# Neighbour rows of a speech codec kernel: 29 transposing loads from HBM replaced by transfers inside SBUF, and new instruction queues

## The chip, the cores and the metric

The kernel runs on one core of one Trainium2 chip. The metric is the device time of one execution in microseconds (us). The engines have these names in the text and in the profile: PE is TensorE (matrix products), DVE is VectorE, ACT is ScalarE, POOL is GpSimd, and SP is SyncE, which here does nothing but issue transfers. HBM is the chip's large memory, SBUF the core's working memory of 128 partitions, PSUM the eight banks that PE writes.

## The reference

A speech codec's core: a three-tap convolution along time for each of 512 channels, SiLU, four rounds of residual vector quantization with eight entries each, and a second three-tap convolution over the sum of the picked entries. `x` is 2 x 16000 x 512 in bf16.

```python
xp = jnp.pad(x, ((0,0),(pad,pad),(0,0)))
z = jnp.zeros_like(x)
for i in range(K):                                   # K = 3
    z = z + xp[:, i:i+T, :] * dw_enc[i][None, None, :]
z = _silu(z)
res = z
q = jnp.zeros_like(z)
for s in range(Nq):                                  # Nq = 4, codebooks of C = 8 rows
    cb = codebooks[s]
    d2 = jnp.einsum("btd,btd->bt", res, res)[..., None] - 2.0 * jnp.einsum("btd,cd->btc", res, cb) + jnp.einsum("cd,cd->c", cb, cb)[None, None, :]
    idx = d2.argmin(-1)
    sel = cb[idx]
    q = q + sel
    res = res - sel
qp = jnp.pad(q, ((0,0),(pad,pad),(0,0)))
y = jnp.zeros_like(x)
for i in range(K):
    y = y + qp[:, i:i+T, :] * dw_dec[i][None, None, :]
return y
```

## The kernel before

**Tiles.** Each of the two sequences is cut into nine tiles (18 in all, numbered 0 to 17). A tile has G groups of 128 rows: G is 6 and 8 for the two tiles at the outer ends and 16 for the rest. Neighbouring tiles overlap by two rows. Partition p of a tile holds the G consecutive rows p*G to p*G+G-1, so that "group g" is the set of rows p*G+g for all p.

**The transposed input and its halo.** The first convolution wants channels on the partitions. So the tile lies transposed in a buffer `XT` of 128 channels x 4 blocks of channels x 18 slots x 128 columns. Slot g+1 holds group g, and column p of a slot is row p*G+g. The tap before group 0 needs the row in front of each p*G, and the tap behind group G-1 the row behind each p*G+G-1. Slot 0 (the halo before) and slot G+1 (the halo behind) hold them. The row in front of p*G is row (p-1)*G+G-1, which is column p-1 of slot G: slot 0 is slot G shifted by one column, and slot G+1 is slot 1 shifted by one column the other way. Only one column of each cannot be had in this way: column 0 of slot 0 and column 127 of slot G+1 are rows outside the tile, which feed only rows that the overlap lets the neighbour tile compute.

**Loading.** Tiles 0 and 1 come by two plain transfers (L569), are turned by PE and copied into `XT1` (L580, L590). Every later tile is loaded by `load`: G transposing transfers from HBM (L599), one for each group, and two for the halo, each a further transposing transfer of the same size from HBM, whose rows start one row earlier (L607, 15 of them) or one row later (L613, 14 of them). Where a tile touches the start or the end of a sequence, POOL makes the halo instead: a fill with zeros (L609, L615) and a copy of the shifted slot (L610, L616). All these transfers are issued by SP. There are two buffers `XT0` and `XT1`, used in turn, so the loads of tile n can start only when the last tap of tile n-2 has read the buffer.

**What follows for a tile.** Each tile is worked in two halves of two channel blocks.
- `front`: the three taps, one multiplication with `WENC` each, on ACT (L640) or DVE (L641) into `TA` and `TB`; two sums on DVE (all DVE operations on two tensors are recorded at L393); exponential on ACT (L646); plus one on ACT (L647) or DVE (L648).
- `front2`: reciprocal on ACT (L658) and the gate product on DVE (L393), which gives `ZB`.
- `select`: PE multiplies `ZB` with the codebooks and itself (L677, 8064 small products); small DVE steps decide the first three entries of every row.
- `resid`: PE subtracts the picked entries from `ZB` in PSUM (L835, L840); copies on ACT (L862) or DVE (L863) bring the result back; scores for the fourth entry and its decision.
- `back`: the second convolution as PE products of one-hot rows with weighted codebooks (L912, L914, L916), copies from PSUM into one of four output buffers `YB` (L921 on ACT, L922 on DVE), and the store (L949), issued by SP.
PE also runs products that nobody reads while it would be idle (L969, "fillers").

**What sets the order.** The program does not issue its steps as the loops go. Each step is given to a class `Plan` with its engine (or a choice of ACT and DVE), an assumed duration ("cost"), the tokens that it reads and writes, and for a transfer a "tail", the assumed time until it has landed. The order on each of the five queues is baked into the string `RANK`, two digits for each step, and the choice between ACT and DVE into the string `WHERE`. `Plan.order` replays the five queues with the assumed costs only to merge them into one sequence and to place the fillers. In that replay a step waits for an earlier one in this way:

```python
end = t + c + s["tail"]
...
at[u] = max(at[u], t + c + self.AGAIN[e] if ue == e else end + self.LATENCY[e])
```

For a step on another engine the tail counts; for a step on the same engine it does not, and `AGAIN["SP"]` is 0. In the built program each queue keeps its order, and every dependence between two engines, or on a transfer, is a semaphore wait of the dependent instruction.

Of the kernel before, what the change touches and what calls it, by code (L numbers as in the profile page):

```python
# [185 lines left out]
def kernel(  # L186
# [33 lines left out]
    RANK = ("00010300000501090M0f0a0N080K0e010b030f0X0l0e0i0b0U0h0q0s000o000q0A0b0d0n0E040s0708020f0a0e060g0109040607090d0f0i0j02080a"  # L220
            "0c0e0g0h0m05050d070709020406040a0c0608010b0i0r03020A0H0K0v050c0T0V0Y1115191b0q0E0F0c0G0r0j0m0o1e1m1p1d1o1u0h0o0t1j1w1y0p"
            "0d0k0m030i0t0z0F0H0J0L0P0S0g0j0l0p0k0v0D0y0I0B0O0x0l130u0m0u0G0w0C0j1i0p1r0n1l0k1g0Q0h0g0R0W100Z120n1f171614181a1h1c1k0w"
            "0z0y1A0B1E0r0s1M1O1N1P1Q1R1S0k0t0L0u1T1V1X1Z1W1Y202122230l0v250w242628292a2b2c2d0n0x0P0y0z2i2j0A0B0T0R0C0D2n2m0E0F0U0V0G"
            "0H2t2A2D2H2J0K120N170P191m0M141t1s1n1q0x1t1x1v1z0D271B1C1D0C1F1G1H1I0J0O0h050b0708030i0g0a0604090c0f020j0l0d1L0I1J1K1U0M"
            "0N2e0Q2l0S2w0W2v0X2x0I0J2z2B2C2E2G2I2K0o0L130O2M2N2O2R2T2W2X2Y2Z300p0Q330R31343637383a3b3c0q0S3e0T0U3i3j0V0W3l1b0X0Y1d3n"
            "0Z101e3o11123t3w3x3z3B151l1c1t1f1u1p191n1a1o1f2h2k2f2g2o2p2q2r102L0t0o0B0u0k0m0e0q0A0n0z0r0p0v0x0s0y0w0Z2s0Y2u2y2F112P16"
            "182U152V2S3239353d1a3p1c3r1g3F1i3E13143D16173I3L3K3N3P3Q3S0r1d1p1g3U3W3Y403V3Z414243440s1i471j464a4c4b4d4e4f4g0u1k1v1l1m"
            "1x1y1n1o1z1A1p1q1D4u1r1s1C4x1v1w4H1x1z4Q4V4X4Z531L1P1S1Y2024211R1X1W221Y1Q1W1Y201Z1P1V1V2627181b3R1e1h3X48454k4l4p4s0t1t"
            "4z1u4v4w4y4A4C4D4E4F4G4I0v1y4L1A4J4K4M4P4R4S4U4W0w1D1J1F1G541M1I1J1O1N1K1M1S1R1N1O1U1T1T1Z5C21225F5H5J5L5O265W29282b2a2f"
            "2a292e2b2u2q2l2A2r2t2r2n2x2q2p0G0O0Q0E0D0T0M0I0N0C0R0F0K0J0P0H0S0L3k3g3h3f3m1f3q3s1k491h3v3u3y3A1j3C3H1q4m15110Y1a0Z0W17"  # L230
            "100V161912181c14130X0U3M3J3O1m3T1r1s4h1w4o1B4B1E4N1G4Y1B1C511E1H565a585c5e5h2Q5j0y1U5s1X5l5n5p5r5w5y5A5E5G5I0z235M245K5N"
            "5R5Q5T5Y60630C2d652f2g2e2d2h2i6e2f2l2m2i2h2n2o2j2k2t2v6C2u2z6L6N6P6T702I732S2G327D2K2L2C2M2E2C2N2D2R2F2F2U2H312O2N4n4i4q"
            "4j4r1F4t4O1K571h1i1b1v1u1s1g1d1r1x1w1o1n1l1e1q1k1j504T1I1H521L55591Q5o5d5f5g5b5i5m5k5q1Z5B215P255Z276425275V282c676b6a6d"
            "6f6h3G6j0D2p6r2s6m6o6q6s6u6v6w6x6y6z0E2w2o2y6A6D6F6E6G6H6I6J0F2B2s2D2F2w2x2G2H2z2v2J2K2A2B2V2Y2K7v33357J38397Q7S7W7Y813g"
            "2W3k303m312W3j2Z3w373b3n323l353d3o8j3q38342j2k6k2C2E6S6W6V7274767a0H2Q7f2T7c7e7g7i7j7k7m7o7q7s0I2Z2J307t7u7y7x7z7A7B7C0J"
            "347F36372P2Q3b3c2U2T3e3f2V2X3h3i2Y893p3r8h3t3v8n8p8r8t8A3G8I413u423w3z3N3l3U3o3r403t3P3v3v3O3m3Q3p3E1C1F1I1E1P1G1A1z1y1O"
            "1M1B1H1N1D1L1K1J5u5v5x5t5z235D5S2c6B625X615U6669686c2g6t1U1X251V1T1R292a1S26222820231Q241W0x0A6l6g6n6i6p2p2m6K2t6X2u752y"
            "772I7H2O2P7d2W2X7n7r7p7w7E7G7I0K3a2R3d7K7M7N7O7V7X7Z8486880L3s343u8b8f8i8l8o8q8s8u0M3x8x3y3z3a3c3C3D3h3d3E3H3i3f3J3K3j3k"
            "3T3V983W3Y9e9j9l9n9q453y4l3L4g3N3M4h3J4p3M3L4d3E4q3Q3Q4s3P4t3S3S6Q6O6M6R6U6Y6Z712M7L2n2d2c2i2e2j2k2l2h2w2m2g2b2q2o2r0B0G"
            "2s787b797h7l2L2N7P2S837R7T807U8285878a338w368y398G3b8H3A3B8F3F3I8K8O8N8Q8S8U8V0N3R8X3S8Y909295919497999a9b0O3X3r3Z9d9f9h"  # L240
            "9g9i9k9m9o0P439r46473z3A484a3C3F4b4c9F3D4e4f3G3H4i4j9R4m4na4a7a9abad4xak4B3U4C3V494A3T4F3X3Y4E3W4Gaz414W484R4c4g3L3M8R44"
            "499y9C9A9E9J9M9O0Q4k9U4o9Q9T9W9Z9Ya3a6aaacae0R4wag4zahajamanaparasau0U4Daw4H4I3Z404J4K41424L4M43464O4PaQ454S4Tb14X4Ybabd"
            "bgbjbn594h5c4k5f4n4E5e4p5n4u4z5g4o5r4A4H5k4r5o4t4B2L2A2I2G2J2E2z2M2y2x2v2D2R2B2Q2P2O2H8d8e8g8c8k8v8m8z3e8M8E8B8C8D8J3g8L"
            "8P3n9c30352Y36372U3a38323c33392S2V312Z2X2T938Z8W8T963s3q9p3x9x3B9H3I9V3Ka14r4uaf4v4yalaqaoataxaBaD0S4NaM4QaGaIaKaNaRaTaU"
            "aVaWaX0T4UaZ4VaYb0b2b3b4b5b6b70W4Z4a5152bi4d55564g4f585a4j4i5b5d4m4l5h5lbK5i5pbNbQbTbVbY5F4G5J4N5P4P4I5I4L5X4U4Q5O4O5S4R"
            "4N5Q4Q5T4T4R9u9s9t9v9w9B9z9D3Oai3l3s3f3h3t3i3g3w3k3u3p3n3o3q3m3e3x3j9L9I9G9K9N9P9S9X3Raya0a5a2a8av3YaAaC44aS47b849bb4bbo"
            "5054bl5357bpbsbrbvbybAbC0V5j4q5mbEbGbIbMbHbLbPbRbWbZ0X5u4x5wc1c3c5c6c7c8c9cb0Z5xcg5y5z4Bck5A5B4E4D5C5D4F4H5G5H4K4J5K5NcD"
            "5M5RcGcKcMcOcV5Zd1634X6f594Z6o5b6q5f506g586n5c516e576j5d525q5sbU5t5vc4cacccdcecfci0Y5E4I5LcmcqcscwcycAcCcEcJcL105WcP5YcN"
            "cRcUcTcWcXcYcZ12614W64654Z5066675251686955546c6d56ds6h6idF6m6pdNdUdWe0e56ye76G5s6S5y536O5v6UeT546M5u6Q5w566F5r6N5t553O3J"
            "3D3N3F3G3H3R3P3U3C3y3B3I3K3A3V3TaEaJaHaFaLaPaOb94ebtbfbebcbhbkbmbqbu4sc03Z4h404f4344424c3W4b4d4e484a4746453XbxbwbBbzbDbJ"  # L250
            "bFbO4vc24zcn4Ccp4McF5U5VcQ6062d3d6d5d9dbdedg136adj6bdidkdmdpdndqdtdvdxdy146kdC6ldzdAdHdGdKdMdPdS166sdV6u6v5h5k6w6x5ie86A"
            "6C5o5n6D6Eel5p6H6Jeu6L6PeFeIeKeMeO6VeW7e5K7m5Q577h5O7n5P587f5L7o5R597c5J7g5N5a4ybXbS4wchclcjco4Sd04o4w4y4x4n4q4r4v4A4u4s"
            "4p4t4l4j4k4m4icvcuctcrcxcBczcH4Ydfd2cS4VcId4d7d8da53dr5adQ5ee25ge66r6tdX6z6Beaefecehekemen176Ieq6KepeteweAevexeBeCeDeE18"
            "6ReG6TeHeJeLeNePeQeReS1b6XeU6Z70f0f67172f25C75765E5G777bfi5I7j7lfB7q7ufQfUfXfYg77Ggd7L5Z7Wgx5d7Kgj7Mgm5b7Q607U645c7S627X"
            "635e6W6YeV7374f3f5f4f7f8f9fb19795H7dfdfgfhfjfkflfmfnfofp1a7i5M7kfqfrfsfvfwfxfyfA1e7pfE7r7tfL5S7w7x5U5T7A7B5W5X7E7Fgc5Y7J"
            "7Ngk7T7ZgygCgGgHgI86gK8ggQ8i6e5h886a8bgN5f8e6c8f6d5g8m6g8n6h5i4K4O4L4J4G4C4D4P4M4FdldcdhdddodudwdB5mejdJdIdEdDdLdRdOdT5q"
            "ey5xeY5zeZ787afeftfufzfCfDe9fF1c7sfK7vfGfHfIfJfMfNfOfPfRfS1d7z5V7CfTfVfWfZg0g2g5g81i7Hgg7P7R61gu8081656682836867848769gL"
            "8h8lgSgTgUgVgW8qgY8v6l8x6m5k8s6j8u6k5j4T4V4S4Y4X4U4W1115e1dZdYe3e45l5jeb5Af1eeeiedegeoeresez5Bfa5Dfc5Fff7y7Dg1g4g3g6g9ga"
            "eXgb1f7Ige7Ogfghgignglgogpgqgrgs1g7Vgw7YgtgvgAgzgBgDgEgF1h85gJ898agM6b8c8dgPgO8j8kgR6f8o8pgX6i8r8tgZh0h1h2h38wh48yh58Ah6"
            "5m8z6n5l")  # L260
# [331 lines left out]

    def load(st):
# [11 lines left out]
        if t0 and n:  # L605
            before = xf[r0 - 1:r0 - 1 + G * P, :].rearrange("(p g) d -> g p d", g=G)[0]
            add("SP", 1.4, ("load", n, 0.01 * G), lambda: nc.sync.dma_start_transpose(out=X[:, :, 0, :], in_=before), [], xe, tail=1.5, after=first_loads if n == EARLY else ())  # L607
        else:
            pool_memset(X[:, :, 0, 0:2], 0.0, xe, 0.3, key)  # L609
            add("POOL", 1.0, key, lambda: nc.gpsimd.tensor_copy(X[:, :, 0, 1:P], X[:, :, G, 0:P - 1]), [("X", st["xb"], G)], xe)  # L610
# [396 lines left out]
```

## Time and profile before

The three runs took 602.18, 603.38 and 601.05 us, median 602.18.

| quantity, profiled execution of before | value |
| --- | --- |
| its own time | 602.52 us |
| its span | 600.7 us |
| PE busy | 500.1 us (83%) |
| DVE busy | 562.4 us (94%) |
| ACT busy | 548.7 us (91%) |
| POOL busy | 53.6 us (9%) |
| mean granted clock of PE | 0.983 of full speed |
| moved by DMA | 71.84 MB in 155564 packets, 146895 of them under 512 B |
| transposing loads issued by SP | 267 |

An engine is "busy" while one of its compute instructions runs; waiting and issuing transfers do not count. SP therefore has no busy time, though its queue can hold work up: how long an issue occupies the queue is read from SP's timeline. In the timelines a row is the start and the length in us, the engine, the line (L599 is line 599 of the kernel before), the operation, what it writes and reads, and how many instructions of that kind follow each other ("x5"). A row that ends in brackets tells how long the engine had been idle before and what released it. A row of the grouped view (`L641 DVE ...`) gives the number of instructions, their busy time and the mean duration in ns, then the idle time just before them with what ended most of it; a row of the DMA issues by place gives the number, then the smallest, median and largest issue time in ns. "By line" in the chain of waits gives the share of a stretch by what the last-ending chain of work was doing; "SPq" is SP's queue issuing.

### The profile page before, as it was taken

The numbers are of one execution on the slowest core, as the hardware profiler recorded it, in microseconds if no ns is written. First come the engines' busy times: TensorE is split into PE (matmuls) and PEld (weight loads), VectorE is DVE, ScalarE is ACT, GpSimd is POOL, SyncE is SP. The second block draws the span as 40 slices with busy tenths as digits, with TensorE's granted clock in tenths as the row PEclk, the third lists the DMA queues.
The fourth block names the chain that finished last, engine by engine and source line by source line (L and its number), as shares of the span: only waits on it lengthen the run. The fifth ranks groups of instructions, "written<-read, shape, count | busy, mean of one in ns | idle before, by whom it ended". The sixth has DMA issues, their size and how long they took to land.

```text
span 600.7 us, 27780 instructions
## 1 busy us (share of the span) xinstructions
PE 500.1 (83%) x12632; PEld 241.1 (40%) x12632; DVE 562.4 (94%) x1125; ACT 548.7 (91%) x419; POOL 53.6 (9%) x86
## 2 busy tenths in 40 slices
PE   4878988888877896878887876888888989999995
PEld 3334434333424343333444343344434344545452
DVE  7999999999999999999999999999999999996764
ACT  4889999999999999999999999999999999996454
POOL 1001010010000101200102000001200200001000
PEclk9888999999999999999999989999999999999999
DMA  9343445475456655794778868665584823044155
GB/s 222 84 93 73 84 102 90 75 133 124 73 97 139 138 117 107 174 155 92 142 140 95 168 123 188 147 108 115 82 179 88 177 56 109 4 144 142 39 183 183
DMA packets 155564, 71.84 MB, mean 120 GB/s; under 512 B 146895, under 2 KB 146927, under 8 KB 155318
## 3 DMA queue, kind: packets, MB, share of 16 engines
q1 hardware_dynamic: 155230, 69.64, 55.3%
q8 instruction: 98, 1.61, 1.1%
q10 hardware_dynamic: 216, 0.43, 0.3%
q14 instruction: 20, 0.16, 0.1%
HBM read 2.26 MB, written 32.77 MB: 58 GB/s over the span
## 4 chain that ended last, share of the span: by engine, by line
DVE 23%; PE 12%; SPq 8%; ACT 8%; issue 5%; DMA 1%; DVEq 0%; ACTq 0%
SPq L599 7%; DVE ZB L393 6%; DVE TB L641 3%; PE banks L835 3%; PE banks L912 3%; PE banks L677 2%; PE banks L840 2%; DVE TA L393 2%; ACT ZB L862 2%; DVE TA L641 2%; ACT EX L646 2%; DVE EX L648 1%; ACT YB L921 1%; DVE ZB L863 1%; DMA XT<-in_x_dram 1%
## 5 line engine op out<-in xcount | busy, mean ns | idle before, releaser
L921 ACT CAST YB<-banks 128x1024 bf16<-128x1024 f32 x115 | 111.6, 1037 | 12.9 <-PE banks L912 6.6
L646 ACT ACTIVATE EX<-ZB 128x4096 bf16<-128x4096 bf16 (+2 forms) x36 | 115.3, 3205 | 4.1 <-DVE ZB L393 3.9
L658 ACT ACTIVATE EX<-EX 128x4096 bf16<-128x4096 bf16 (+2 forms) x36 | 115.1, 3201 | 0.1
L862 ACT CAST ZB<-banks 128x1024 bf16<-128x1024 f32 (+2 forms) x109 | 97.7, 952 | 16.3 <-PE banks L840 16.3
L969 PE MATMUL banks<-MSK,IDENT 128*128 128x512 bf16 x413 | 103.5, 392 | 6.4 <-issue 2.6
L677 PE MATMUL banks<-ZB 128*32 128x64 bf16 x8064 | 90.4, 197 | 9.7 <-issue 6.0
L677 PEld LDWEIGHTS <-ZB 128*32 128x32 bf16 x8064 | 75.6, 95 | 52.6 <-issue 44.7
L912 PE MATMUL banks<-WDEC,OHW 128*128 128x512 bf16 x252 | 74.0, 382 | 14.3 <-ACT ZB L862 8.0
L840 PE MATMUL banks<-OHR,WR 32*128 32x512 bf16 (+2 forms) x1152 | 81.6, 355 | 0.1
L641 DVE TENSOR_SCALAR TB<-XT,WENC 128x2048 bf16<-128x2048 bf16 (+2 forms) x115 | 76.7, 676 | 1.6 <-issue 1.2
L393 DVE TENSOR_TENSOR ZB<-TA,TB 128x4096 bf16<-128x4096 bf16 (+2 forms) x36 | 73.0, 2028 | 0.8 <-ACT TB L640 0.4
L393 DVE TENSOR_TENSOR TA<-TA,TB 128x4096 bf16<-128x4096 bf16 (+2 forms) x36 | 72.7, 2020 | 0.5
L393 DVE TENSOR_TENSOR ZB<-ZB,EX 128x4096 bf16<-128x4096 bf16 (+2 forms) x36 | 72.3, 2017 | 0.3 <-ACT EX L658 0.2
L835 PE MATMUL banks<-ZB,IDENT 64*64 64x512 bf16 (+2 forms) x576 | 54.3, 368 | 13.4 <-DVE ZB L863 3.0
L749 POOL COPY OHD<-OHA 128x256 bf16<-128x256 bf16 (+2 forms) x36 | 27.5, 764 | 417.3 <-DVE OHA L393 417.3
L969 PEld LDWEIGHTS <-IDENT 128*128 128x128 bf16 x413 | 38.4, 100 | 49.7 <-issue 13.8
L640 ACT ACTIVATE TB<-XT,WENC 128x2048 bf16<-128x2048 bf16 (+2 forms) x29 | 53.2, 1845 | 3.6 <-DVE TA L393 2.0
L835 PE MATMUL banks<-ZB,UP 64*64 64x512 bf16 (+2 forms) x576 | 52.4, 353 | 0.0
L840 PEld LDWEIGHTS <-WR 32*128 32x128 bf16 x1152 | 23.4, 92 | 58.3 <-issue 50.1
L641 DVE TENSOR_SCALAR TA<-XT,WENC 128x2048 bf16<-128x2048 bf16 (+2 forms) x66 | 44.0, 676 | 1.5 <-DMA XT<-in_x_dram 1.4
L835 PE MATMUL banks<-ZB,DOWN 64*64 64x512 bf16 (+2 forms) x576 | 41.4, 363 | 0.0
L863 DVE CAST ZB<-banks 128x1024 bf16<-128x1024 f32 (+2 forms) x35 | 32.8, 950 | 7.3 <-PE banks L840 7.3
(133 smaller groups left out, 580.9 us busy)
## 6 DMA issues: line engine op xcount, KB each, us to landing
out_dram<-YB SPq DMA_DIRECT2D x33, 448.0 KB
out_dram<-YB SPq DMA_DIRECT2D x28, 512.0 KB
XT<-in_x_dram SPq DMA_TRANSPOSE x267
out_dram<-YB SPq DMA_DIRECT2D x30, 60.0 KB
...
out_dram<-YB SPq DMA_DIRECT2D x31, 2.0 KB
...
```

Of the source, the lines that this page charges most:

```text
L393: add("DVE", cost, key, lambda: nc.vector.tensor_tensor(out=out, in0=a, in1=b, op=op), reads, writes, **kw)
L640: either({"ACT": act(R), "DVE": dve(R, 3.84) + 0.06}, key, lambda dst=dst, src=src, w=w: nc.scalar.mul(dst, src, w), lambda dst=dst, src=s ...
L641: lambda dst=dst, src=src, w=w: nc.vector.tensor_scalar(out=dst, in0=src, scalar1=w, scalar2=None, op0=ALU.mult),
L646: add("ACT", act(2 * R), ("exp", n, h), lambda: nc.scalar.activation(v(ex), Z, ACT.Exp, scale=-1.0), zt, [("EX", sl), "ACTTAB"], hold="E")
L658: nc.scalar.add_instruction(mybir.InstActivation(name=nc.get_next_instruction_name(), engine=mybir.EngineType.Activation, func=ACT.Reciprocal,
L677: nc.tensor.matmul(o[HB * q:HB * (q + 1), u * ZW:(u + 1) * ZW].rearrange("p (s c) -> p s c", s=2), lhsT=blk, rhs=both, start=False, stop=( ...
L835: nc.tensor.matmul(at(r)[to], lhsT=dia[h, h], rhs=Z[h, i, r:G:RG, :], start=start, stop=False)
L840: nc.tensor.matmul(at(r), lhsT=WR[v][g, i * P:(i + 1) * P], rhs=W[g, v // 3, 0:rows_of[r], :], start=False, stop=stop)
L862: either({"ACT": act_psum(2 * k * P), "DVE": dve(2 * k * P)}, key(1), lambda dst=dst, src=src: nc.scalar.copy(dst, src()), lambda dst=dst, ...
L912: nc.tensor.matmul(o, lhsT=W[:, k, PADC:PADC + P], rhs=WDEC[u], start=True, stop=not wrap)
L921: either({"ACT": act_psum(1024), "DVE": dve(1024)}, key, lambda dst=dst, box=box: nc.scalar.copy(dst, ps(box)), lambda dst=dst, box=box: n ...
L969: nc.tensor.matmul(PS[j // 2][:, 512 * (j % 2):512 * (j % 2) + NMK * ZW], lhsT=IDENT, rhs=MSK.rearrange("p u w -> p (u w)"), start=True, s ...
```

## The change

Three things are changed.

1. In `load`, the halo slots of tiles 2 and later are no longer loaded from HBM. SP issues a plain transfer from one slot of `XT` to another, shifted by one column: 128 partitions x 4 blocks x 127 columns. It reads slot G (or slot 1), which transposing loads of the same queue write, and carries that dependence. At the ends of a sequence POOL's fill and copy stay.
2. Since these transfers leave column 0 of slot 0 and column 127 of the last slot alone, POOL fills these two columns of `XT0` once at the start.
3. The planner's tail of the two first loads is changed from 2.4 + 0.3 G (4.2 and 4.8 us) to 5.8 and 7.6 us, and `RANK` and `WHERE` are replaced as a whole, so all queues have a new order and some steps a new engine.

```diff
-    RANK = ("00010300000501090M0f0a0N080K0e010b030f0X0l0e0i0b0U0h0q0s000o000q0A0b0d0n0E040s0708020f0a0e060g0109040607090d0f0i0j02080a"
...
+    RANK = ("000104000d0c000e0f090H0h0b0L0a0J0i010h0g0f0n0x0i0q0e0v0d0W0t00070c0f0j0C0M0l0z030i010w0h0D0g0t0I0V000202040607080a0j0l01"
...
-        first_loads.append(add("SP", 0.6, ("load", n, 0), lambda: nc.sync.dma_start(out=rows, in_=src), [], [("STAGE", n)], tail=2.4 + 0.3 * G))
+        first_loads.append(add("SP", 0.6, ("load", n, 0), lambda: nc.sync.dma_start(out=rows, in_=src), [], [("STAGE", n)], tail=5.8 if n == 0 else 7.6))
...
+    for g, c in ((0, 0), (GM + 1, P - 1)):
+        pool_memset(XT[0][:, :, g, c:c + 1], 0.0, [("XE", 0) if g == 0 else ("X", 0, g)], 0.3, ("pad", -20, 0))
+
     def load(st):
...
         if t0 and n:
-            before = xf[r0 - 1:r0 - 1 + G * P, :].rearrange("(p g) d -> g p d", g=G)[0]
-            add("SP", 1.4, ("load", n, 0.01 * G), lambda: nc.sync.dma_start_transpose(out=X[:, :, 0, :], in_=before), [], xe, tail=1.5, after=first_loads if n == EARLY else ())
+            add("SP", 0.55, ("load", n, 0.01 * G), lambda: nc.sync.dma_start(out=X[:, :, 0, 1:P], in_=X[:, :, G, 0:P - 1]), [("X", st["xb"], G)], xe, tail=2.5)
...
         if t0 + G * P < T and n:
-            behind = xf[r0 + 1:r0 + 1 + G * P, :].rearrange("(p g) d -> g p d", g=G)[G - 1]
-            add("SP", 1.4, ("load", n, 0.01 * G), lambda: nc.sync.dma_start_transpose(out=X[:, :, G + 1, :], in_=behind), [], xo, tail=1.5, after=first_loads if n == EARLY else ())
+            add("SP", 0.55, ("load", n, 0.01 * G), lambda: nc.sync.dma_start(out=X[:, :, G + 1, 0:P - 1], in_=X[:, :, 1, 1:P]), [("X", st["xb"], 1)], xo, tail=2.5)
```

In the lines of the kernel after, everything from L593 on moves by one to three lines: the two halo transfers are L609 and L614 there, the transposing loads L602, the taps L641 (ACT) and L642 (DVE), the stores L950.

More of the change, by code (lines that the diff above doesn't have):

```diff
@@ L219 @@
     DIGITS = "0123456789abcdefghijklmnopqrstuvwxyzABCDEFGHIJKLMNOPQRSTUVWXYZ"
-    RANK = ("00010300000501090M0f0a0N080K0e010b030f0X0l0e0i0b0U0h0q0s000o000q0A0b0d0n0E040s0708020f0a0e060g0109040607090d0f0i0j02080a"
[L221 to L260, printed above, removed]
@@ new lines @@
+    WHERE = ("DADDAAAAADAAAAAAADDDDDDDDDDAAADADAADADDAAAADDDDDDADDDADDADADDADDADADADADDAAAAAAADDDDDDADADADAADDDDDDDADAADAAADADAAAAAAAA"
+            "AADAAAAAAAAADAAAAAAAADDDDDDDADDAADDDDDAAADDDDAAAAAAAADAAAAAAAADDDDADDDDAADADDDDDDDDDDADAAAAAAAAAAAAAADADDAAAAAAAAADAAAAA"
+            "AAADDDDDDDDDDDDDDDDDDAADDADAADAAAAADAAAAAAAADDDDDDDADDDDDDDDDDDDDDADAAAAAAAADAAAAADAADDDAAAAAADADAAAAAAAADDDDDDDDDDDDADD"
+            "DADADDDDAAAAAAAAAAAAAAAAAADDDDDDDDDDDDDDDDDDADDAADADAAAAADAAAAAAAAAADAAADAAADDDADAAAAAADDDDDDDDDDDADDDDDDDDDDDDAAAAAAADD"
+            "AAAAAAAAADDDDDDDDDADDDDDDADDDDDDADDADAAADDAADAADADDDAADAAADADDAAADDAADDDDDDDDDDDDDDAAAADAAADADDDDDADDDDDDDDDDDADDDDDAADA"
+            "AAAAAAAA")
```

46 lines of the change are left out of this document (40 added, 6 removed).

## The prediction

> **What bounds the kernel now.** I read the page's head, then busy time by stage, then the chain of waits and the SyncE queue.
>
> ```profile
> span 600.7 us, 27780 instructions
> PE 500.1 (83%) x12632; PEld 241.1 (40%) x12632; DVE 562.4 (94%) x1125; ACT 548.7 (91%) x419; POOL 53.6 (9%) x86
> ```
>
> ```profile
> 0.00:25.00 25.00, 14.66 (x106) 8.81 (x107) 20.58 (x89) 14.91 (x32) 1.83 (x25) 0.93 0.69 165
> 25.00:515.00 490.00, 407.75 (x10300) 193.58 (x10298) 480.83 (x863) 476.89 (x327) 47.90 (x50) 0.99 0.60 117
> 515.00:601.00 86.00, 77.67 (x2255) 38.75 (x2237) 61.00 (x176) 56.91 (x62) 3.88 (x11) 0.98 0.35 121
> ```
>
> The columns are the stretch, its length, then the busy time of PE, PEld, DVE, ACT and POOL. In the 490 us between the set-up and the last taps DVE is busy 480.83 and ACT 476.89: both are the bound, and either may lose only 9 to 13 us. In the last 86 us PE is (77.67), in the first 25 the loads. There is a third party, the SyncE queue (SP), which the busy table does not count:
>
> ```profile
> by line: SPq L599 60.4%; DMA XT<-in_x_dram 10.7%; SPq L949 7.3%; SPq L613 4.6%; DVE ZB L393 3.4%; issue 3.1%; ACT TB L640 2.9%; ACT ZB L862 2.9%; SPq L607 2.4%; DVE ZB L863 1.7%; DVE TB L641 1.2%; DVEq L641 0.1%
> ...
> 305.62 2.99 DMA XT<-in_x_dram
> ...
> 337.21 3.94 DMA XT<-in_x_dram
> ```
>
> This is the chain between 280 and 345 us: three quarters of it are SP issuing (L599, L607 and L613 transposing loads, L949 stores). So SP's time is not free. Tile 12 shows how tight it is:
>
> ```profile
> 311.51 7.44 SPq L599 DMA_TRANSPOSE XT<-in_x_dram  x5
> 318.99 1.73 SPq L613 DMA_TRANSPOSE XT<-in_x_dram  x1
> 320.77 10.52 SPq L599 DMA_TRANSPOSE XT<-in_x_dram  x7
> 331.38 0.53 SPq L949 DMA_DIRECT2D out_dram<-YB  x1
> 331.95 4.59 SPq L599 DMA_TRANSPOSE XT<-in_x_dram  x3
> 336.64 0.52 SPq L949 DMA_DIRECT2D out_dram<-YB  x1
> 337.21 1.52 SPq L599 DMA_TRANSPOSE XT<-in_x_dram  x1
> 338.77 1.28 SPq L607 DMA_TRANSPOSE XT<-in_x_dram  x1
> ...
> 437.44 2.10 SPq L599 DMA_TRANSPOSE XT<-in_x_dram  x1
> ```
>
> ```profile
> 309.48 2.00 ACT L640 ACTIVATE TB<-XT,WENC 128x2048 bf16<-128x2048 bf16 x1
> ```
>
> ```profile
> 342.42 0.75 DVE L641 TENSOR_SCALAR TB<-XT,WENC 128x2048 bf16<-128x2048 bf16 x1
> ...
> 448.30 0.74 DVE L641 TENSOR_SCALAR TB<-XT,WENC 128x2048 bf16<-128x2048 bf16 x1
> ```
>
> Tile 10's last tap ends at 309.48 + 2.00 = 311.48 and frees the buffer; 18 loads and two stores take SP from 311.51 to 340.05; the first tap of tile 12 starts at 342.42, 2.4 us behind. For tile 15 (last two rows) that distance is 8.8. Read in the same way, tiles 4 to 16 have 2.5, 2.6, 6.9, 3.8, 3.6, 3.1, 6.1, 5.8, 2.4, 2.3, 4.8, 8.8 and 6.1. Landing comes off that:
>
> ```profile
> 235.31 2.97 SPq L599 DMA_TRANSPOSE XT<-in_x_dram  x2
> ```
>
> ```profile
> 239.82 2.63 POOL L610 COPY XT<-XT 128x508 bf16<-128x508 bf16 x1 [9.54 <-DMA XT<-in_x_dram]
> ```
>
> The second transpose was issued by 238.28 and POOL, waiting for it, started at 239.82: 1.5 us. The chain's 305.62 row is 2.99 for the same thing beside other traffic. I take 2.2. So tiles 4, 5, 12 and 13 have no spare, 8 has 1.4, 7 has 1.6 and the others 0.9 to 6.6.
>
> **The change, part by part.**
>
> *Halos, SP's account.* 29 transposing loads go, 29 plain transfers come.
>
> ```profile
> L607 SPq DMA_TRANSPOSE XT<-in_x_dram x15: 1202/1265/2149, 30.8 to 478.2; - x15
> ```
>
> ```profile
> L613 SPq DMA_TRANSPOSE XT<-in_x_dram x14: 1194/1265/1733, 17.4 to 444.8; - x14
> ```
>
> ```profile
> 7.58 0.36 ACTq L378 DMA_DIRECT2D YB<-in_dw_dec_dram  x1
> ```
>
> Removed: 29 x 1.27 = 36.8 us. No row has a plain transfer with three steps on both sides (128 partitions x 4 x 127 elements). Its issue lies between 0.36 (plain, rows in one piece) and 1.27 (512 pieces, transposed); I take 0.7, nearer the plain rows (the stores above take 0.52): 20.3, ends 10.4 and 36.8. Then there is an added wait. The transfer reads a slot that a transpose has just been asked to fill, so SP must wait for that landing, and every later load and store is queued behind it. In the built order 15 of the 29 stand directly behind their source, one stands two places behind and two stand three; for 11 the source is four or more places back and has landed. 15 x 2.2 = 33 us, ends 15 x 1.5 = 22.5 and 15 x 2.99 = 45; about 1 for the one at two places. SP's account: -36.8 + 20.3 + 34 = +17.5 us, ends -4 and +46. The file's planner books no wait between two steps of one queue, so its order counts on less SP time than before, not more.
>
> The Trainium skill speaks against this part: "DMA: Bandwidth & Descriptors", section "Two DMAs through the same engine are not ordered", says that a dependent DMA has to wait for the first one's completion semaphore on its issuing engine, the same queue being no substitute. The wait in the built order agrees. The same page (section "Anatomy of one DMA") gives about 2.0 us of fixed cost for a DMA, measured on GpSimd's path; at that price, an estimate, the 15 waits would be 30 us and the five tiles below would lose 2.2 us less, which makes the sum 603.8.
>
> *What of it reaches the taps.* Per tile, two halos with no waiting transfer give SP 2 x (0.7 - 1.27) = -1.1 us, with one +1.1, with two +3.3. Against that stands the vector work that the new order puts between the buffer's last tap and the tile's first one (instructions of the built order by the mean durations of this trace), and stores moved among the tiles (0.5 each). Tile 4: two waiting, +3.3, window +2.1 (28.5 to 30.6), spare 0.3: late by 0.9. Tile 7: +1.1, window -1.3, spare 1.6: 0.8. Tile 8: its one halo waits, -1.27 + 0.7 + 2.2 = +1.6, window -1.6, spare 1.4: 1.8. Tile 12: +1.1 and six stores more (+3.0), window +1.4, spare 0.2: 2.5. Tile 13: +1.1, six stores fewer (-3.0), window -4.2, spare 0.1: 2.2. The others keep a spare: 5 has a wider window, 9 and 10 have no waiting transfer, 6, 11, 14, 15 and 16 lose less than they had. Sum 8.2 us; DVE and ACT stand 97 to 98% full, so nothing gives it back. Ends: 0 (landing 1.5 and issue 0.36 leave every tile on time), and 20, the same five sums with 1.27, 2.99 and the spares less 0.8 (3.9, 3.5, 4.0, 4.6 and 4.2).
>
> ```profile
> 116.99 0.75 DVE L641 TENSOR_SCALAR TA<-XT,WENC 128x2048 bf16<-128x2048 bf16 x1 [1.35 <-DMA XT<-in_x_dram]
> ```
>
> This wait of tile 5 goes (its window grows by 2.3): -1.4.
>
> *Work changes engine.*
>
> ```profile
> L921 ACT CAST YB<-banks 128x1024 bf16<-128x1024 f32 x115 | 111.6, 1037 | 12.9 <-PE banks L912 6.6 <-PE banks L916 3.3 <-DVE ZB L863 2.1
> ...
> L862 ACT CAST ZB<-banks 128x1024 bf16<-128x1024 f32 x93 | 89.9, 1027 | 12.4 <-PE banks L840 12.4
> ...
> L641 DVE TENSOR_SCALAR TB<-XT,WENC 128x2048 bf16<-128x2048 bf16 x88 | 65.1, 747 | 1.5 <-issue 1.2
> ...
> L640 ACT ACTIVATE TB<-XT,WENC 128x2048 bf16<-128x2048 bf16 x24 | 48.0, 2014 | 3.4 <-DVE TA L393 2.0 <-DMA XT<-in_x_dram 1.4
> ...
> L648 DVE TENSOR_SCALAR EX<-EX 128x4096 bf16<-128x4096 bf16 x27 | 33.1, 1224 | 0.2 <-ACT EX L646 0.2
> ...
> L863 DVE CAST ZB<-banks 128x1024 bf16<-128x1024 f32 x19 | 23.1, 1216 | 2.6 <-PE banks L840 2.6
> ```
>
> Counts become L641 91, L640 21, L863 17, L862 95, L921 114 (L922 on DVE 12 for 11), L648 26 with L647 on ACT 2 for 1 (about 3.6 each). Taps: +2.2 on DVE, -6.0 on ACT; residue copies -2.4 and +2.1; outputs +1.2 and -1.0; plus-one -1.2 and +3.6. The smaller forms, each priced by its own mean, give -4.0 on DVE and +4.8 on ACT (512-wide residue copies, one 2048-wide plus-one, set-up, turned one-hots). Sum: DVE -4.2 us, ACT +3.5. If DVE alone were the bound the span would fall by 4.2, if ACT alone it would rise by 3.5. The page's chain has DVE at three times ACT (23% against 8%), so I weigh them 3 to 1: -2.3.
>
> *First loads.* Only a planner's figure changes; the two loads are issued as before.
>
> ```profile
> 9.00 0.69 DVE L590 COPY XT<-banks 128x1024 bf16<-128x1024 bf16 x1 [2.89 <-PE banks L580]
> ```
>
> DVE idles 2.9 us until tile 0 is there. The new order has 43 vector instructions before that copy where there were 46, and 4.8 us of work for 4.9, so the hole stays. What can go are later waits (DVE idles 4.4 of the first 25, ACT 10.1): between 0 and -2.5; I take -1. If it went wrong it would cost what the set-up now spread to 35 us delays, up to +1.
>
> *Without price.* Two POOL fills of one column (about 0.1 us each) at the start, under POOL's 9%; fillers on PE 413 to 411; the tail after the last gate has the same matmuls within two per tile and 2 us less vector work under a PE that is the bound there: 0, were PE not the cover -2. Stores queued behind the waits come later by up to 3 us; four output buffers cover that, else ACT's L921 would wait.
>
> Sum: the profiled execution took 602.5 us (span 600.7 and 1.8 around it), +8.2 - 1.4 - 2.3 - 1.0 = 606.0. The median of the runs, 602.2, is 0.3 below that execution. What a measurement of this kernel can tell from no change is about 0.5%, 3 us.
>
> **Rivals.**
>
> *The order wins (faster).* If landing takes 1.5 and issue 0.36, SP's account is -4 and no tile is late; with -1.4, -2.3 and -1 the time is 597.8. For it: 11 transfers wait for nothing, and most windows hold 32 us or more. Against: tiles 4, 7, 8, 12 and 13 were at 0 to 1.6 of spare. It decides when fewer than about two tiles come late. 0.22.
>
> *The waits hide and the exchange is worth nothing (no change).* ACT's 13 us of idle time fill with the 3.5 it gets, DVE's saving only lengthens its waits for ACT, and late tiles cost the 2.4 that tile 5 and the first loads give: 602.5. Both are within 1% of each other in the middle stage, which speaks for it. 0.26.
>
> *The transfers land late (much slower).* Each moves 512 pieces of 254 bytes at odd addresses.
>
> ```profile
> DMA packets 155564, 71.84 MB, mean 120 GB/s; under 512 B 146895, under 2 KB 146927, under 8 KB 155318
> ```
>
> Nearly all packets are short already, and those of the transposes land in 1.5 to 3, which speaks against. With the five tiles at their upper ends the time is 602.5 + 20 - 4.7 = 618; were landing 5 us, tiles 2 and 14, whose last entry is such a transfer, would lose 3 each, 624. The near end, half way from the forecast, is 612. 0.12. The Trainium skill's "DMA: Bandwidth & Descriptors", section "Specifications", says that below 512 B a transfer is done by read-modify-write; no row here separates that.
>
> **How the numbers follow.** My forecast (one to three more tiles late or not: 603 to 609) has 0.40, of which 0.32 lie above 605.2 and 0.08 below. Slower: 0.32 + 0.12 = 0.44; same: 0.26 + 0.08 = 0.34; faster: 0.22. The range must take in most of the faster rival and the near end of the slow one: 596 to 614.
>
> **What would show it.** In the new profile: SP waits for XT's own loads at the two halo lines, some 15 of 1.5 to 3 us; SP's issue of a transfer near 0.7; taps of tiles 4, 7, 8, 12 and 13 waiting for XT, together 5 us or more on DVE or ACT against 1.4 now; DVE near 558, ACT near 552; PE's tail unchanged. The prediction is wrong if the taps do not wait (then 598 to 602), if ACT's busy share does not rise, or if taps wait for the transfers themselves rather than for the loads behind them.

## The result and the profile after

The kernel after takes 606.38 us (median of 20 runs, 602.78 to 614.17), the kernel before 603.43 us beside it (median of 20 runs, 600.55 to 606.29). The ratio is 1.0051, with a 95% interval of 1.0031 to 1.0070: slower by 3.1 us. The forecast was 606.0 against 602.5, 3.5 us more. The single runs of the kernel after spread over 11 us, those of before over 6, and the profiled execution of after is one of its quick ones (603.42 us, span 601.6). So its rows tell where time goes, and the runs tell how much.

The head of the page of the kernel after:

```profile
span 601.6 us, 27790 instructions
PE 503.8 (84%) x12630; PEld 242.5 (40%) x12630; DVE 559.1 (93%) x1120; ACT 552.6 (92%) x424; POOL 53.5 (9%) x88
```

Busy time of PE, PEld, DVE, ACT and POOL by stage:

```profile
0.00:25.00 25.00, 12.56 (x93) 8.11 (x94) 19.14 (x88) 15.10 (x34) 1.82 (x27) 0.90 0.69 170
25.00:515.00 490.00, 411.77 (x10220) 195.27 (x10220) 478.75 (x856) 478.86 (x327) 45.69 (x49) 0.96 0.58 117
515.00:602.00 87.00, 79.45 (x2341) 39.09 (x2327) 61.18 (x178) 58.62 (x65) 5.95 (x12) 0.99 0.36 120
```

DVE has lost 3.3 us of work and ACT has got 3.9. In the 490 us of the middle both now stand at the same 479. The last stage is still PE's.

SP's own waits, each row with the sum, the number of times and the longest:

```profile
SPq L609 <- DMA XT<-in_x_dram: 18.7, 10, 3.2
SPq L614 <- DMA XT<-in_x_dram: 7.4, 6, 1.5
```

The two halo lines and their issue (number, then smallest, median and largest time in ns):

```profile
L609 SPq DMA_DIRECT2D XT<-XT x15: 603/605/948, 30.6 to 480.3; - x15
```

```profile
L614 SPq DMA_DIRECT2D XT<-XT x14: 594/622/2001, 13.5 to 459.7; - x14
```

SP waits 16 times, 26.1 us together, for loads that it has itself just issued. A transfer inside SBUF costs its queue 0.6 us, where the transposing load cost 1.27. Tile 12 on SP's timeline, the stretch that the prediction showed of before:

```profile
311.82 10.96 SPq L602 DMA_TRANSPOSE XT<-in_x_dram  x7
324.29 0.63 SPq L614 DMA_DIRECT2D XT<-XT  x1
325.01 2.15 SPq L950 DMA_DIRECT2D out_dram<-YB  x3
...
341.33 1.28 SPq L950 DMA_DIRECT2D out_dram<-YB  x3
342.66 5.79 SPq L602 DMA_TRANSPOSE XT<-in_x_dram  x4
```

The seventh load is issued by 322.78, the halo transfer behind it only at 324.29: 1.5 us in which SP does nothing. The tile's last load, the first of the group at 342.66, is issued by 344.5, 32.8 us after the buffer came free, against 28.6 before. What the taps make of it, the DVE taps that waited for a transfer:

```profile
178.52 0.75 DVE L642 TENSOR_SCALAR TB<-XT,WENC 128x2048 bf16<-128x2048 bf16 x1 [1.20 <-DMA XT<-in_x_dram]
214.16 0.75 DVE L642 TENSOR_SCALAR TA<-XT,WENC 128x2048 bf16<-128x2048 bf16 x1 [2.36 <-DMA XT<-in_x_dram]
347.08 0.75 DVE L642 TENSOR_SCALAR TB<-XT,WENC 128x2048 bf16<-128x2048 bf16 x1 [1.44 <-DMA out_dram<-YB]
449.45 0.75 DVE L642 TENSOR_SCALAR TB<-XT,WENC 128x2048 bf16<-128x2048 bf16 x1 [0.97 <-DMA XT<-in_x_dram]
```

These are the first taps of tiles 7, 8, 12 and 15: 6.0 us of DVE's time, against 1.35 before (tile 5). ACT has one such wait in each trace: 1.1 us at tile 15, and 1.4 us before, at tile 5. The third row is put down to a store because that was the last semaphore to come; the tile's last load was issued 2.6 us ahead of it.

### The profile page after: what moved, and what is told of

Same layout as the page of the kernel before. It is cut to its first block, busy times and chain, and to the rows that moved or that the text cites. A ratio compares the mean times of both kernels' runs of the same rounds, so it can differ in the third digit from the quotient of the medians.

```text
span 601.6 us, 27790 instructions
## 1 busy us (share of the span) xinstructions
PE 503.8 (84%) x12630; PEld 242.5 (40%) x12630; DVE 559.1 (93%) x1120; ACT 552.6 (92%) x424; POOL 53.5 (9%) x88
## 4 chain that ended last, share of the span: by engine, by line
DVE 27%; ACT 21%; SPq 21%; PE 15%; DMA 10%; issue 7%; ACTq 0%; DVEq 0%
SPq L602 17%; DMA XT<-in_x_dram 8%; DVE ZB L393 5%; ACT EX L659 5%; PE banks L836 4%; DVE TB L642 4%; DVE TA L393 4%; ACT YB L922 3%; ACT EX L647 3%; ACT TB L641 3%; PE banks L913 3%; PE banks L841 3%; DVE TA L642 3%; SPq L950 2%; ACT ZB L863 2%
## 5 line engine op out<-in xcount | busy, mean ns | idle before, releaser
L863 ACT CAST ZB<-banks 128x1024 bf16<-128x1024 f32 (+2 forms) x115 | 101.1, 938 | 21.0 <-PE banks L841 18.0
L922 ACT CAST YB<-banks 128x1024 bf16<-128x1024 f32 x114 | 111.3, 1033 | 9.1 <-PE banks L913 5.7
L970 PE MATMUL banks<-MSK,IDENT 128*128 128x512 bf16 x411 | 106.0, 393 | 8.0 <-issue 6.0
L678 PEld LDWEIGHTS <-ZB 128*32 128x32 bf16 x8064 | 77.3, 97 | 58.5 <-issue 43.3
L642 DVE TENSOR_SCALAR TB<-XT,WENC 128x2048 bf16<-128x2048 bf16 (+2 forms) x120 | 79.6, 673 | 4.0 <-DMA XT<-in_x_dram 2.2
L750 POOL COPY OHD<-OHA 128x256 bf16<-128x256 bf16 (+2 forms) x36 | 34.6, 960 | 458.9 <-DVE OHA L393 439.9
L836 PE MATMUL banks<-ZB,IDENT 64*64 64x512 bf16 (+2 forms) x576 | 56.0, 365 | 12.6 <-DVE OHR L793 2.6
L642 DVE TENSOR_SCALAR TA<-XT,WENC 128x2048 bf16<-128x2048 bf16 (+2 forms) x65 | 43.9, 685 | 2.5 <-DMA XT<-in_x_dram 2.4
L641 ACT ACTIVATE TB<-XT,WENC 128x2048 bf16<-128x2048 bf16 (+2 forms) x24 | 45.0, 1883 | 1.1 <-DMA XT<-in_x_dram 1.1
L671 PE MATMUL banks<-MSK,IDENT 128*128 128x512 bf16 (+1 forms) x64 | 25.6, 400 | 16.4 <-ACT CB L495 12.8
```

The lines of the kernel that those rows point to most:

```text
L642: lambda dst=dst, src=src, w=w: nc.vector.tensor_scalar(out=dst, in0=src, scalar1=w, scalar2=None, op0=ALU.mult),
L678: nc.tensor.matmul(o[HB * q:HB * (q + 1), u * ZW:(u + 1) * ZW].rearrange("p (s c) -> p s c", s=2), lhsT=blk, rhs=both, start=False, stop=( ...
L836: nc.tensor.matmul(at(r)[to], lhsT=dia[h, h], rhs=Z[h, i, r:G:RG, :], start=start, stop=False)
L863: either({"ACT": act_psum(2 * k * P), "DVE": dve(2 * k * P)}, key(1), lambda dst=dst, src=src: nc.scalar.copy(dst, src()), lambda dst=dst, ...
L922: either({"ACT": act_psum(1024), "DVE": dve(1024)}, key, lambda dst=dst, box=box: nc.scalar.copy(dst, ps(box)), lambda dst=dst, box=box: n ...
L970: nc.tensor.matmul(PS[j // 2][:, 512 * (j % 2):512 * (j % 2) + NMK * ZW], lhsT=IDENT, rhs=MSK.rearrange("p u w -> p (u w)"), start=True, s ...
```

## The experiments

Each experiment ran beside the kernel before on the same chip: experiments 1 to 4 on one, 5, 6, 7 and 9 on a second, 8, 10 and 11 on a third. So the ratios are what to compare. Of the theories that the expectations name, W says that SP's waits make the loads behind them late, O that the new queues themselves cost the time, and T that the transfers inside SBUF land late or disturb other loads.

**1. No waits, everything else as after.** A few lines ahead of the ordering rearrange SP's queue alone: the load that a halo transfer reads is moved ahead among the loads of its tile, and the transfer back where that is not enough.

```diff
...
+    def place(least):
+        sp = sorted((s["n"] for s in reversed(plan.steps) if s["e"] == "SP"), key=lambda n: plan.ranks[n])
+        for copy, source, loads in halos:
+            first, at = min(map(sp.index, loads)), sp.index(copy)
+            if sp.index(source) > max(first, at - least - 1):
+                sp.remove(source)
+                sp.insert(max(first, at - least - 1), source)
+            if sp.index(copy) < sp.index(source) + least + 1:
+                sp.remove(copy)
+                last = max(map(sp.index, loads))
+                sp.insert(min(sp.index(source) + least, last) + 1, copy)
+        for r, n in enumerate(sp):
+            plan.ranks[n] = r
+
+    place(4)
```

> The kernel after, with SP's queue alone rearranged so that every halo transfer stands at least three, most of them five, SP instructions behind the transposing load that it reads; nothing else changes. Theory W (SP's waits for its own loads make the loads behind them late): the 26.1 us of SP waits at the halo transfers fall below 5, the waits of the taps for XT fall from 7.0 us to 3 or less, and of the 3 us by which the kernel after is slower 3 to 5 come back: 601 to 603.5. Theory O (the new queues themselves, the work that changed engine and the later first copies, cost the 3 us, and SP's waits are hidden): the SP waits go and the time stays at 605.5 to 607. Theory T (the transfers inside SBUF land late or disturb the other loads): the time stays at 605.5 to 607 too, and taps still wait for XT.

Measured: 602.20 against 602.95, ratio 0.9993 (0.9970 to 1.0015). SP's waits for its loads are gone altogether, and of the taps' waits one of 1.1 us is left. The whole slowdown comes back, 0.58% or 3.5 us. W holds, O and T fall.

DVE's queue is the same in both programs, instruction for instruction, so the two traces can be laid side by side. The four first taps that came late start here as follows (the taps on DVE are L645 in this kernel):

```profile
177.54 0.75 DVE L645 TENSOR_SCALAR TB<-XT,WENC 128x2048 bf16<-128x2048 bf16 x1 [0.20 <-issue]
...
210.84 0.75 DVE L645 TENSOR_SCALAR TA<-XT,WENC 128x2048 bf16<-128x2048 bf16 x1
...
343.57 0.75 DVE L645 TENSOR_SCALAR TB<-XT,WENC 128x2048 bf16<-128x2048 bf16 x1 [1.12 <-DMA out_dram<-YB]
...
446.97 0.75 DVE L645 TENSOR_SCALAR TB<-XT,WENC 128x2048 bf16<-128x2048 bf16 x1
```

In the kernel after, DVE lags by 1.0, 3.3, 3.5 and 2.5 us at these taps and by 1.8 us at its last instruction. The late taps add 4.7 us, and 2.9 of them come back at other places, mostly where DVE waits for PE or ACT here and not in the kernel after. This is one pair of executions.

**2. The exchange undone, the new queues kept.**

```diff
-            add("SP", 0.55, ("load", n, 0.01 * G), lambda: nc.sync.dma_start(out=X[:, :, 0, 1:P], in_=X[:, :, G, 0:P - 1]), [("X", st["xb"], G)], xe, tail=2.5)
+            before = xf[r0 - 1:r0 - 1 + G * P, :].rearrange("(p g) d -> g p d", g=G)[0]
+            add("SP", 1.4, ("load", n, 0.01 * G), lambda: nc.sync.dma_start_transpose(out=X[:, :, 0, :], in_=before), [], xe, tail=1.5, after=first_loads if n == EARLY else ())
...
```

> The kernel after with its queues, but the 29 halo slots again by transposing loads from HBM at the same places of SP's queue, without waits for their source. SP gains 26.1 us of waits and loses 29 x (1.27 - 0.605) = 19.3 us of issue, so 7 us net. Theory W: about a quarter of the taps' extra waits goes, 605 to 606.5. Theory O: the same as after, 605.5 to 607. Theory T: the whole difference goes, 602 to 604.

Measured: 602.92 against 602.95, ratio 1.0002 (0.9978 to 1.0025). W is right in kind (T is out by experiment 1), but my figure for it was wrong: SP gains only 7 us here, and still the whole 3 us come back. The cost is not proportional to SP's time. The run says a second thing: the new queues by themselves, with the halos of before, are worth nothing, where the prediction gave them 4.7 us.

**3. The exchange without waits, in the queues of before.** The same lines of rearrangement and the two halo transfers put into the kernel before; the two border columns are filled ahead of everything.

```diff
-            add("SP", 1.4, ("load", n, 0.01 * G), lambda: nc.sync.dma_start_transpose(out=X[:, :, 0, :], in_=before), [], xe, tail=1.5, after=first_loads if n == EARLY else ())
+            c = add("SP", 0.55, ("load", n, 0.01 * G), lambda: nc.sync.dma_start(out=X[:, :, 0, 1:P], in_=X[:, :, G, 0:P - 1]), [("X", st["xb"], G)], xe, tail=2.5)
+            halos.append((c, loads[G - 1], loads))
...
+    place(4)
...
+        for g, c in ((0, 0), (GM + 1, P - 1)):
+            nc.gpsimd.memset(XT[0][:, :, g, c:c + 1], 0.0)
```

> The kernel before with its queues, and the 29 halos by transfers inside SBUF, each at least three, most of them five or more, SP instructions behind its source. SP gets 29 x (1.27 - 0.605) = 19.3 us less of issue and hardly a wait. Theory W: the taps' waits for XT stay at 1.4 us or fall, and the time is that of before or up to 3 us less: 600 to 603.5. Theory O: the same as before, 602.5 to 604.5, because the queues are those of before. Theory T: slower than before, 605 to 608.

Measured: 600.82 against 602.95, ratio 0.9963 (0.9942 to 0.9984): faster than both kernels. Its page:

```profile
span 598.9 us, 27799 instructions
PE 502.6 (84%) x12630; PEld 241.7 (40%) x12630; DVE 562.6 (94%) x1125; ACT 549.1 (92%) x419; POOL 56.1 (9%) x88
```

DVE and ACT do the work of before, no tap waits for a transfer, and SP's waits list holds no load. So placed, with nothing behind a wait, the transfers inside SBUF are good for 2.2 us.

**4. The planner's figure for the first loads put back.**

```diff
-        first_loads.append(add("SP", 0.6, ("load", n, 0), lambda: nc.sync.dma_start(out=rows, in_=src), [], [("STAGE", n)], tail=5.8 if n == 0 else 7.6))
+        first_loads.append(add("SP", 0.6, ("load", n, 0), lambda: nc.sync.dma_start(out=rows, in_=src), [], [("STAGE", n)], tail=2.4 + 0.3 * G))
```

> The kernel after with the planner's old figure for the two first loads (4.2 and 4.8 us): the queues keep their order, only PE's fillers at the start can differ. Theories W and T: no change, 605.5 to 607. Theory O, in the form that fewer fillers at the start lower the granted clock (0.84 between 25 and 100 us against 0.95 before): faster than after by 1 us or more, 602 to 605, with a clock near 0.95 in that stretch.

Measured: 606.38 against 602.95, ratio 1.0048 (1.0026 to 1.0071), the result of the kernel after over again. The figure alone changes no instruction, on any engine, so this is a second trace of the same program; its profiled execution took 608.15 us, 4.7 more than the first. Its waits:

```profile
SPq L609 <- DMA XT<-in_x_dram: 22.3, 10, 3.2
SPq L614 <- DMA XT<-in_x_dram: 9.8, 6, 2.1
```

```profile
DVE TA L642 <- DMA XT<-in_x_dram: 3.6, 2, 1.9
DVE TB L642 <- DMA XT<-in_x_dram: 2.7, 2, 1.7
ACT TB L641 <- DMA XT<-in_x_dram: 1.8, 1, 1.8
DVE TB L642 <- DMA out_dram<-YB: 1.0, 1, 1.0
```

The same 16 waits take 32.1 us instead of 26.1, 2.0 each instead of 1.6, and the taps wait 7.3 us on DVE instead of 6.0. The first tap of tile 14 waits too (1.7 us), which it did not in the first trace. How long a load takes to land differs from execution to execution; in this kernel that difference goes into SP's queue. The taps' 1.3 us are only part of the 4.7 between the two executions. The granted clock that the form of O spoke of (0.84 between 25 and 100 us) was the same 0.84 in experiment 1, which is as quick as the kernel before, so it is not the cause.

**5 and 6. Which waits count.** The kernel after, with the rearrangement of experiment 1 for four tiles only, and for all others only (the edits are against experiment 1):

```diff
-        for copy, source, loads in halos:
+        for copy, source, loads, n in halos:
+            if n not in (7, 8, 12, 15):
+                continue
```

```diff
+            if n in (7, 8, 12, 15):
+                continue
```

> The kernel after; only the five waiting halo transfers of tiles 7, 8, 12 and 15, the tiles whose taps waited, are put five places behind their source; the other ten waits stay. Theory W with a threshold (a wait of SP costs only where the tile has no spare left): nearly all that the rearranged queue won comes back, 602 to 603.5, and the taps' waits on DVE fall from 6.0 us to 2 or less. Theory W in proportion (each of the waits costs the same, 4.2 us / 15 = 0.28): 606.4 - 5 x 0.28 = 605.

> The opposite: in the kernel after the ten waiting halo transfers of all other tiles are put apart from their source, and the five of tiles 7, 8, 12 and 15 stay directly behind it. Theory W with a threshold: those tiles are still late, 605 to 606.5, the taps' waits on DVE stay at 4 us or more. Theory W in proportion: 606.4 - 10 x 0.28 = 603.6.

Measured on one chip: the four tiles mended, 600.79 against 601.19, ratio 0.9980 (0.9958 to 1.0002); the others mended, 604.99, ratio 1.0060 (1.0038 to 1.0083). SP's waits in the two, the first with four tiles mended, the second with the others mended:

```profile
SPq L610 <- DMA XT<-in_x_dram: 12.4, 7, 3.1
SPq L616 <- DMA XT<-in_x_dram: 4.3, 3, 1.5
```

```profile
SPq L610 <- DMA XT<-in_x_dram: 5.5, 3, 2.3
SPq L616 <- DMA XT<-in_x_dram: 5.2, 2, 3.2
```

The ten waits that are left in the first cost 16.7 us of SP's time and nothing of the kernel's. The five in the second cost 10.7 us of SP's and all of the slowdown, 4.8 us more than the first. A wait of SP costs only where the tile behind it has no spare left; proportion is refuted. One expectation missed: in the profiled execution of the second the taps on DVE waited only 2.2 us, not 4 or more. That execution took 602.47 us, 2.5 less than the median of its runs. The twelve runs of the first spread over 4.8 us and those of the second over 8.1, so the wider spread of the kernel after may come from the same waits; that is not shown.

**7. A larger dose.** In the queues of before, every halo transfer directly behind its source (the edit is against experiment 3):

```diff
         for copy, source, loads in halos:
-            first, at = min(map(sp.index, loads)), sp.index(copy)
...
+            sp.remove(copy)
+            sp.insert(sp.index(source) + 1, copy)
```

> The queues of before with the transfers inside SBUF, every one of the 29 directly behind its source: the dose of waits is nearly doubled. SP's account: 29 x (26.1 / 16 = 1.63) = 47 us of waits, less 19.3 of issue, +28 us. Theory W with a threshold: tiles 4, 5, 12 and 13, which had 0.1 to 0.4 us of spare, come 1.5 to 2 us late each, 7 and 8 up to 0.5: 7 us more than the same queues with the transfers apart (600.8), 606 to 609. Theory O (SP's waits are hidden, the order decides): 600 to 603.

Measured: 626.07 against 601.19, ratio 1.0408 (1.0378 to 1.0437), 24.5 us slower, where W said 606 to 609. SP's waits, and the waits of DVE and ACT for transfers:

```profile
SPq L607 <- DMA XT<-in_x_dram: 29.4, 15, 3.3
SPq L613 <- DMA XT<-in_x_dram: 28.9, 14, 2.9
```

```profile
ACT YB L922 <- DMA out_dram<-YB: 7.4, 3, 3.7
DVE TA L642 <- DMA XT<-in_x_dram: 5.1, 3, 2.1
DVE TB L642 <- DMA out_dram<-YB: 4.5, 1, 4.5
ACT TB L641 <- DMA XT<-in_x_dram: 3.1, 1, 3.1
DVE TB L642 <- DMA XT<-in_x_dram: 2.1, 1, 2.1
DVE YB L923 <- DMA out_dram<-YB: 1.7, 1, 1.7
DVE TA L642 <- DMA XT<-XT: 1.3, 1, 1.3
```

29 waits take 58.3 us, 2.0 each, so SP's account is +39 us and not +28. More than that, the waits do not stay in the four tiles that I counted (4, 5, 12 and 13): the first taps of tiles 3, 5, 7, 9, 12 and 16 wait for transfers, by 1.1 to 4.5 us, and that of tile 13 does not (tile 4's waits 2.1 us, for what the trace does not name). SP gets to some tiles late (to the loads of tile 8 4.7 us after their buffer came free, against 1.6 before), and the stores that stand behind the waits in the same queue give the four output buffers back late, so ACT's copies (L922) wait 7.4 us. In the queues of before the price of SP's time rises with the dose: with the waits of experiment 8 (17.3 us) nothing is lost, with 58.3 us 24.5. A price taken at a small dose is no price for a larger one.

**8. The exchange as it comes, in the queues of before.** As experiment 3, each transfer at the place of the load that it replaces:

```diff
-    place(4)
+    place(0)
```

> The exchange alone, without new queues: the queues of before, each transfer inside SBUF at the place of the transposing load that it replaces (the few that stood ahead of their source right behind it). 15 of the 29 then stand two places behind their source and 2 directly behind it. SP: 19.3 us less of issue, waits of about 1.6 us twice and 0.4 to 0.8 us fifteen times, so 5 to 10 us less. Theory W with a threshold: no tile is later than before, 600.5 to 603. Theory T (the transfers themselves are slow): 604 or more.

Measured: 601.72 against 603.29, ratio 0.9982 (0.9959 to 1.0006). SP waits 11 times, 17.3 us, so it wins only 2 us where 5 to 10 were expected (in the built order 17 transfers, not 15, stand two places behind their source). No tap is late by more than 1.5 us. Without new queues the exchange does no harm; it was the new order that put 15 transfers directly behind their sources.

**9. The halos as copies on POOL.** As experiment 3, but POOL copies the shifted slot (about 3 us behind the source in the planner's order).

```diff
-            c = add("SP", 0.55, ("load", n, 0.01 * G), lambda: nc.sync.dma_start(out=X[:, :, 0, 1:P], in_=X[:, :, G, 0:P - 1]), [("X", st["xb"], G)], xe, tail=2.5)
+            c = add("SP", 0.55, ("load", n, 0.01 * G), lambda: nc.gpsimd.tensor_copy(X[:, :, 0, 1:P], X[:, :, G, 0:P - 1]), [("X", st["xb"], G)], xe, tail=2.5)
...
+            s["e"], s["c"], s["tail"] = "POOL", 0.7, 0.0
...
```

> The queues of before, with the 29 halos as copies on POOL (as at the ends of the sequences), each put into POOL's queue 3 us behind its source by the planner's clock. SP loses 29 x 1.27 = 36.8 us, POOL gets 29 x 0.65 = 19 us. Theory W: as good as the transfers put apart or better, 599 to 601.5. Against it, theory P (POOL waits for landings, and its copies of the one-hot rows behind them, for which DVE and PE wait, come late): 602 to 606.

Measured: 605.44 against 601.19, ratio 1.0060 (1.0040 to 1.0080). Slower, and not as P said: in the list of waits neither PE nor DVE nor ACT waits for POOL (six loads of SP do, 4.7 us together). Its page's engine line, and the largest tap group with the two groups of halo copies:

```profile
PE 489.6 (81%) x12540; PEld 240.5 (40%) x12632; DVE 568.3 (94%) x1125; ACT 549.7 (91%) x419; POOL 91.3 (15%) x117
```

```profile
L642 DVE TENSOR_SCALAR TB<-XT,WENC 128x2048 bf16<-128x2048 bf16 x88 | 67.0, 769 | 0.3
...
L613 POOL COPY XT<-XT 128x508 bf16<-128x508 bf16 x14 | 24.2, 1729 | 61.8 <-DMA XT<-in_x_dram 39.7 <-DVE TB L642 22.1
L607 POOL COPY XT<-XT 128x508 bf16<-128x508 bf16 x15 | 15.6, 1038 | 20.6 <-DMA XT<-in_x_dram 20.6
```

DVE has the same 1125 instructions as in experiment 3 and is busy 5.7 us longer (568.3 against 562.6); its taps take 769 ns where the trace of before has 747. So DVE itself is slower while POOL copies. The Trainium skill, page "SBUF — State Buffer", section "Who interferes with whom", says that DVE and GpSimd share one pair of ports, which one of them holds for a whole instruction while the other is blocked. The trace agrees:

```profile
318.85 0.67 POOL L613 COPY XT<-XT 128x508 bf16<-128x508 bf16 x1
...
443.23 7.16 POOL L613 COPY XT<-XT 128x508 bf16<-128x508 bf16 x1 [1.42 <-DVE TB L642]
```

```profile
318.97 1.09 DVE L642 TENSOR_SCALAR TA<-XT,WENC 128x2048 bf16<-128x2048 bf16 x1
```

This tap, which starts beside a copy, takes 1.09 us, and the same instruction 0.74 in experiment 3. The other way round, a copy, which takes 0.67 us in the first row, takes 7.16 in the second, where three operations of DVE on two tensors (2.28 us each) run at the same time.

**10 and 11. What a us of work on DVE and on ACT costs.** The prediction weighed them 3 to 1. The kernel before, with small operations in a scratch tile that nobody waits for:

```diff
...
+            for _ in range(3 if s["k"][0] == "gate" and s["k"][2] == 0 else 0):
+                nc.vector.tensor_scalar(out=JUNK, in0=JUNK, scalar1=1.0, scalar2=None, op0=ALU.mult)
```

```diff
...
+            for _ in range(2 if s["k"][0] == "recip" and s["k"][2] == 0 else 0):
+                nc.scalar.copy(JUNK[:, 0:320], JUNK[:, 0:320])
```

> The price of work on DVE, which the prediction set at three quarters: the kernel before, with three small multiplications in a scratch tile (128 x 448, about 0.24 us each) on DVE behind the first gate of every tile, 54 in all, about 13 us of DVE work that nobody waits for. Weights 3 to 1 (DVE is the bound most of the time): +9.8 us, 611 to 614. Equal weights of a half: +6.5, 608 to 611. Both engines on the path nearly everywhere: +11 to +13, 613 to 616.

> The same price for ACT, which the prediction set at one quarter: two small copies in a scratch tile (128 x 320, about 0.37 us each) on ACT behind the first reciprocal of every tile, 36 in all, about 13 us. Weights 3 to 1: +3.3 us, 605 to 607. Equal weights of a half: +6.5, 608 to 611. Both engines on the path nearly everywhere: +11 to +13, 613 to 616. If the two prices are alike, the exchange of work (DVE -3.3, ACT +3.9) is worth nothing, as the kernel after with HBM halos (1.0002) suggests.

Measured: with the work on DVE 614.42 against 603.29, ratio 1.0193 (1.0162 to 1.0225), 11.6 us; with the work on ACT 617.43, ratio 1.0238 (1.0206 to 1.0269), 14.4 us. The engine lines of the two pages, DVE's first:

```profile
PE 506.1 (83%) x12632; PEld 242.4 (40%) x12632; DVE 575.5 (94%) x1179; ACT 550.3 (90%) x419; POOL 53.1 (9%) x87
```

```profile
PE 510.5 (83%) x12632; PEld 243.2 (39%) x12632; DVE 564.7 (92%) x1125; ACT 563.2 (91%) x455; POOL 52.6 (9%) x87
```

DVE got 13.1 us (575.5 - 562.4), ACT 14.5 (563.2 - 548.7). So at these places of each tile a us on DVE costs 0.89 us (0.75 to 1.04 by the interval of the ratio) and one on ACT 0.99 (0.86 to 1.12). That both engines are on the path nearly everywhere fits this; a price of one quarter for ACT does not.

## Why the prediction was right

The time (606.0 forecast, 606.38 measured), the sign and the likeliest case came out, and the mechanism is the one named: SP waits at the halo lines, what is queued behind comes late, and a few taps wait. That the sum came within 0.4 us is luck: its loss (+8.2) and its gains (-4.7) were both too large by about 4.7 us, and they cancel.

- *SP's issue.* 0.7 us taken, 0.6 measured: right in size.
- *SP's waits.* 15 to 16 waits of 2.2 us forecast; 16 waits of 1.6 in one execution and 2.0 in another. With 29 x 0.6 = 17.4 of issue the account is -36.8 + 17.4 + 26 to 32 = +7 to +13 us, against +17.5. The rule of the Trainium skill that was cited (page "DMA: Bandwidth & Descriptors", section "Two DMAs through the same engine are not ordered") shows as those very waits, and they go where the transfers stand apart.
- *Late taps, +8.2.* The mechanism holds, the term was mis-sized: taking SP's waits away gave 3.5 us (experiment 1), and the waits of tiles 7, 8, 12 and 15 alone make 4.8 (experiments 5 and 6). Tiles 7, 8 and 12 were named rightly, at 0.8, 1.8 and 2.5 where the first trace has 1.2, 2.4 and 1.4. Tiles 4 and 13 did not wait in either trace. Tile 4's two waits on SP took 1.5 us each in the first trace, not 2.2. Tile 13's took 1.9; its loads kept SP 3.3 us less than before, where 1.9 were forecast, and its window shrank by 3.2 and not by 4.2. Tile 15 did wait: the new order gave it two waiting transfers and moved stores ahead of its last loads, and its 8.8 us of distance shrank to 3.2. The landing, taken as 2.2 for all, differs from tile to tile: from the issue of the last load to the tap that waited for it 1.7 us (tile 7), 3.8 (8), 2.6 (12) and 3.2 (15). And "nothing gives it back" does not hold: beside experiment 1, 4.7 us of late taps end as 1.8.
- *Tile 5, -1.4.* Its wait is gone, as forecast.
- *Work changes engine, -2.3.* This step failed. Busy times came out as forecast (DVE 559.1 for 558, ACT 552.6 for 552), but the weights of 3 to 1, read from the engines' shares in the chain of waits, were wrong. With the measured prices the exchange is worth -3.3 x 0.89 + 3.9 x 0.99 = +0.9. That both engines stood at 97 to 98% in the middle was a sign of it.
- *First loads, -1.* Wrong sign at its place: DVE's first copy of the input starts at 9.86 us instead of 9.00, and DVE idles 5.9 of the first 25 us instead of 4.4.
- *The three gains together* were to bring 4.7 us; the new queues with the halos of before bring 0.1 the other way, with an interval from 1.3 us of gain to 1.5 of loss (experiment 2).
- *Rivals.* "The order wins" would have given 597.8; without any wait the new order gives 602.2 (experiment 1), so it falls even on its own terms. "The waits hide" is true of ten waits in fifteen (experiment 5). "The transfers land late" falls by experiment 3.

Not settled: how much of the 3.1 us the four tiles share out among themselves, and why the queues without waits of experiments 1 and 5 stay at the time of before, though they hold the same gain for SP as experiment 3. The intervals of these three overlap.
